# Sliding-window attention and a ReGLU layer: v's second copy by transfers over the sync queue, one more product on GpSimd, and other due times for early work

## The chip, the cores and the metric

The kernel runs on one core of a Trainium2 chip. The metric is the device time of one execution in microseconds (us). Before the change it is 318.4 us, the median of three runs (318.24 to 318.41).

A core has a matrix engine (TensorE, PE in the profile), a vector engine (DVE), an engine for activations (ACT), a general one (GpSimd, POOL in the profile), and a sync engine (SP) that here only issues transfers. Each works through its own queue in order and waits for the others at semaphores. Matrix products land in PSUM, of which there are eight banks of 128 x 512 float32.

## What is computed

Batch 8, 8 heads, 576 positions, head size 64. Every position looks at itself and the 63 before it. The result, 4608 tokens of 512 values, goes through a ReGLU layer of width 1536.

```python
def _attn_ref(q, k, v):
    scores = scale * np.matmul(q, k.transpose(0, 1, 3, 2))
    mask = (rel >= 0) & (rel < 64)
    scores = np.where(mask, scores, -1000000000.0)
    ...
    return np.matmul(attn, v)

def _moe_ref(x, w_gate, w_val, w_out):
    gate = np.maximum(x @ w_gate, 0.0)
    val = x @ w_val
    return gate * val @ w_out
```

## The kernel before

**Tiles.** The 4608 tokens are cut into four narrow tiles of 384 (tiles 0 to 3) and six wide ones of 512 (tiles 4 to 9). For each tile the kernel computes attention, turns it into `xt` (features on partitions), computes the hidden layer into `g_sb`, and multiplies by `wo` into the output, 128 rows at a time.

**The order of the work** is written out by a planner, `Weaver`. It has a clock that is advanced by the estimated time of the matrix products as they are emitted, and a heap of pieces of work with due times: `W.at(t, fn)`. Each `W.advance` emits all that is due. `W.pop` emits the earliest piece before its time, where a product needs its result. So due times set only the order in each engine's queue; on the chip an engine runs an instruction as soon as its queue and its inputs allow. A function that is called from the heap and adds to the clock itself (`scores`, `values` in the heap) leaves no trace in the clock, because `pop` writes back its own sum: the planner's clock falls behind there.

**Attention.** `qk_load` brings q and k of a batch and half of the heads on GpSimd's queue, with a cast to fp16; `qk_trans` transposes them on DVE, 128 x 576 each, four for a batch (names `kT`, `qT`). Each of the four has one staging buffer, so a load waits for the transpose of the batch before. `plan_batch(b, load, trans)` plans both. Narrow tiles have units of 192 positions (`u_st`, `u_exp`, `u_mask`, `u_pv`: scores on TensorE, exp on ACT, mask on DVE, value products on TensorE); `pair` plans the two units of a tile. Wide tiles have quads of four windows (`scores`: scores, exp and mask) and `values` (value products, reciprocal, norm and transpose on DVE, and `x_form`, differences of blocks of `xt`, on GpSimd and DVE). For a wide tile, `values` of the next tile run between the output blocks of this one, and `scores` of the tile after that as well.

**v.** `v16s` holds two batches of v in fp16, in groups of 64 positions, each head with 64 values and two ones (66 in all). A window of 64 queries needs the 128 positions that end with it, so every half of 64 rows is needed at partitions 0 to 63 in one group and at 64 to 127 in another. `v_load` brings each half once (GpSimd's queue, with a cast), and `v_spread` copies it to the other partitions: two copies for each unit of 192 positions, on DVE (units 0 and 3) or GpSimd (all others). `v_ahead` and `loads` plan them.

**Hidden layer, narrow tiles (`hidden`).** Gate and value products into one bank each, ReLU on ACT, multiply on DVE.

**Hidden layer, wide tiles (`fast_hidden`).** Blocks of two by two are multiplied with seven products (P1 to P7) instead of eight, from sums of the weights (`us`, `vs`, made once by `w_form` on GpSimd) and of the inputs (`xc`). Three rounds j of 14 products (seven for the gate, i = 0, and seven for the value, i = 1), 42 steps of four matrix instructions. P1, P6, P7 and P4 add up in one bank A, in this order; after each of the first three `snap` copies the bank to SBUF on ACT (L594), and the next product into A has to wait for this copy. P2, P5 and P3 go to other banks, and `add` sums them to the copies on DVE (L604). P3 waits for the sum with P7. Each finished pair gets a ReLU on ACT (L610) and a multiply on GpSimd (L615). These copies live in six buffers `pr`, each with a gate and a value half, taken in turn: three for a round. The fourth quarter, which is A after P4, goes by `direct`: ReLU on ACT into a buffer `r` (L624), and a multiply on DVE that reads the value half straight from PSUM (L633).

**Output.** `fast_output` multiplies `g_sb` with `wo` for four blocks of 128 rows (12 matrix instructions each, L676), with attention of later tiles between them; ACT copies each block to `o_sb`, and SP writes it out (L683; L699 in narrow tiles). For the first two blocks it reads the half h = 0 of `g_sb`, which has the fourth quarters of each round first.

Of the kernel before, what the change touches and what calls it, by code (L numbers as in the profile page):

```python
# [10 lines left out]
FP32 = mybir.dt.float32  # L11
FP16 = mybir.dt.float16
ACT = mybir.ActivationFunctionType
MUL = mybir.AluOpType.mult
# [33 lines left out]
def kernel(  # L48
# [10 lines left out]
    nc = tc.nc  # L59
# [12 lines left out]
    WT = 512  # L72
    NS = 4
# [12 lines left out]
    f_sb = ctx.enter_context(tc.tile_pool(name="f_sb", bufs=3))  # L86
# [6 lines left out]
    wv = persist.tile([128, NC, DF], FP16)  # L93
    wo = persist.tile([128, NF, DM], FP16)
    HF = NF // 2
# [42 lines left out]
    W = Weaver()  # L138
# [32 lines left out]
    def qk_load(b, name, hh):  # L171

        tile_ = nat[b, name, hh] = a_in.tile([128, S // 32 * D], FP16, name=f"{name}{hh}")
        src = (q if name == "q" else k)[b, G * hh:G * hh + G]
        nc.gpsimd.dma_start(tile_, src.rearrange("h (i j) d -> (h i) (j d)", i=32))
# [14 lines left out]
    def qk_trans(b, name, hh, j0=0, j1=S // 32):  # L190

        src = nat[b, name, hh].bitcast(FP32).rearrange("p (j e) -> p j e", e=32)
        dst = qTs[b % 2][:, hh] if name == "q" else kTs[b % 2][:, hh, 64:64 + S]
        dst = dst.bitcast(FP32).rearrange("p c o -> p (c o)")
        nc.vector.transpose(dst.rearrange("p (i j) -> p j i", i=32)[:, j0:j1], src[:, j0:j1])
# [8 lines left out]
    def v_spread(u, copy=None, h0=0, h1=H):  # L204

        b, uu = divmod(u, UB)
        t = v16s[b % 2]
        copy = copy or nc.vector.tensor_copy
        for g0, g1 in (((0, 3),), ((4, 5),), ((6, 7),))[uu]:
            copy(t[64:128, g0:g1:2, h0:h1, 0:64], t[0:64, g0 + 1:g1 + 1:2, h0:h1, 0:64])  # L210
        for g0, g1 in (((2, 3),), ((4, 5),), ((6, 9),))[uu]:
            copy(t[0:64, g0:g1:2, h0:h1, 0:64], t[64:128, g0 - 1:g1 - 1:2, h0:h1, 0:64])

    def heat(n, to, start=True):

# [57 lines left out]
    def u_st(u, hhs=(0, 1)):  # L273
        d = units.setdefault(u, {})
        if "st" not in d:
            st_tiles(u)
        run_rows([[st_block(d["st"][g][:, U * hh + 64 * w:U * hh + 64 * w + 64], g, hh, UB * u + w, "biased" in d)
                   for hh in hhs for w in range(UB)] for g in range(G)])
        return 0.29 * len(hhs)
# [42 lines left out]
    def u_recip(u, hhs=(0, 1)):  # L322
        d = units[u]
        if "r" not in d:
            d["r"] = a_n.tile([128, 2, SB, 1], FP32, name="r")
        for hh in hhs:
            nc.vector.reciprocal(d["r"][:, hh], pv_of(d, u, hh)[:, :, D:D + 1])
# [36 lines left out]
    free = []  # L364
# [111 lines left out]
    def w_form(wt, n, j):  # L476

        to = us if wt is wg else vs
        c = slice(256 * j, 256 * j + 256)
        f = slice(256 * j + 128 * HF, 256 * j + 128 * HF + 256)  # L480
        a11, a12, a21, a22 = wt[:, 0:2, c], wt[:, 2:4, c], wt[:, 0:2, f], wt[:, 2:4, f]
        x, y, op = ((a21, a22, ADD), (to[:, 0, :, c], a11, SUB), (a11, a21, SUB), (a12, to[:, 1, :, c], SUB))[n]
        nc.gpsimd.tensor_tensor(to[:, n, :, c], x, y, op)

    def plan_batch(b, load, trans):
        for i, (name, hh) in enumerate((n, hh) for n in "kq" for hh in range(2)):
            if load is not None:
                W.at(load, lambda name=name, hh=hh: qk_load(b, name, hh))
            W.at(trans[i], lambda name=name, hh=hh: qk_trans(b, name, hh))

    def plan_exps(T, u, mask=True, gap=0.4, first=0.8):
        for i in range(G):
            W.at(T + first + gap * i, lambda i=i: u_exp(u, i))
            if mask:
                W.at(T + first + 0.45 + gap * i, lambda i=i: u_mask(u, i))
# [54 lines left out]
    def fast_hidden(t):  # L550

        g_sb, done = gs[t] = g_sb_p.tile([128, NF, WT], FP16, name="g_sb"), {}
        xt, xc = xt_tile(t), xcs[t]
        b11, b21, b22 = xt[:, 0:2, 0:HT], xt[:, 2:4, 0:HT], xt[:, 2:4, HT:WT]
        gh = g_sb.rearrange("p f (h n) -> p f h n", h=2)
        pair = lambda ap: ap.rearrange("p (f n) -> p f n", f=2)
        kinds = ((wg, us), (wv, vs))
        at = {}
# [60 lines left out]

        def direct(j, i):  # L620
            if i == 0:
                def relu():
                    at[j, "r"] = f_sb.tile([128, WT], FP32, name="r", bufs=2)
                    nc.scalar.activation(at[j, "r"], at[j, "A", 0], ACT.Relu)  # L624
                    free.append(at[j, "A", 0])
                    at[j, "relu"] = True
                W.at(W.clock, relu)
            else:
                def mult():
                    while (j, "relu") not in at:  # L630
                        W.pop()
                    f = 2 * j + HF
                    nc.vector.tensor_tensor(gh[:, f:f + 2, 0], pair(at[j, "r"]), pair(at[j, "A", 1]), MUL)  # L633
                    free.append(at[j, "A", 1])
                    done[f, 0] = done[f + 1, 0] = True
                W.at(W.clock + 0.2, mult)

        def step(j, name):
            for i in range(2):
# [97 lines left out]
    with tc.manual_schedule():  # L737
        G3, V3, O3 = ([(wt, src, f0, f0 + 4) for f0 in (0, 4, 8)]
                      for wt, src in ((wg, moe_w_gate), (wv, moe_w_val), (wo, moe_w_out)))
        act, dve, pool = nc.scalar.copy, nc.vector.tensor_copy, nc.gpsimd.tensor_copy  # L740
# [81 lines left out]
        def pair(t, TA, TB, P):  # L822
            for u, T in ((2 * t, TA), (2 * t + 1, TB)):
                W.at(T, lambda u=u: u_st(u))
                plan_exps(T, u)
            W.at(P, lambda: u_pv(2 * t) + u_pv(2 * t + 1))
            for n in range(2):
                u = 2 * t + n
                W.at(P + 0.7 + 1.7 * n, lambda u=u: u_recip(u))
                for hh in range(2):  # L830
                    W.at(P + 0.9 + 0.5 * hh + 1.7 * n, lambda u=u, hh=hh: u_norm(u, hh))
                W.at(P + 1.9 + 1.7 * n, lambda u=u: u_turn(u))

        def loads(t, T):
            for u in (2 * t, 2 * t + 1):
                b, uu = divmod(u, UB)
                if uu == 0:
                    plan_batch(b, T - 12.0, (T, T + 1.4, T + 2.8, T + 4.2))
                W.at(T - 6.0, lambda u=u: v_load(u))
                W.at(T + 1.0, lambda u=u: v_spread(u, pool))  # L840

        for u in (4, 5):
            W.at(52.0, lambda u=u: v_spread(u, pool))
        pair(2, 55.5, 58.5, 61.9)
        L_T = 3 * 6.53
        WIDE_T = L_T + 13.1
# [1 line left out]
        def batch_of(t):  # L848
            w0 = q_window(2 * (t - NS), 0)
            b = (w0 + 2 * QW - 1) // NG  # L850
            return b, w0 <= NG * b

        def qk_ahead(t, T, gaps, lead=12.0):
            b, new = batch_of(t)
            if new:
                plan_batch(b, T - lead, [T + x for x in gaps])

        def v_ahead(t, T):
            b, new = batch_of(t)
            us = list(range(UB * b, UB * b + UB)) if new else []  # L860
            if t == NS:
                us.insert(0, UB * b - 1)
            for i, u in enumerate(us):
                W.at(T - 5.0, lambda u=u: v_load(u))
                W.at(T + 6.0 + 2.5 * i, lambda u=u: v_spread(u, pool))

        LAST = NS + NL - 1
        SLOTS = (2.6, 6.53 + 0.8, 6.53 + 2.6, 2 * 6.53 + 0.8)

        def ahead(t):  # L870
            T = W.clock
            if t + 1 < NS:
                pair(t + 1, T + 11.0, T + 14.0, T + 17.5)
            if t == NS - 2:
                qk_ahead(NS, T + 20.5, (0.0, 1.5, 3.0, 4.5))
                v_ahead(NS, T + 27.0)
                for j in range(NF // 4):
                    for n, at in enumerate((0, 1, 3, 2)):
                        W.at(T + 12.0 + 6.4 * j + 1.6 * n, lambda at=at, j=j: w_form(wv, at, j))
            if t == NS - 1:  # L880
                qk_ahead(NS + 1, T + 11.5, (0.0, 1.4, 8.0, 9.4))
                for qd, x in ((0, 6.0), (1, 9.2), (2, 22.6), (3, 25.8)):
                    def st(qd=qd):
                        scores(qd, W.clock, two_banks() + two_banks(), qd == 3)
                    W.at(T + x, st)
                for hh in range(2):
                    def pv(hh=hh):
                        values(NS, hh, W.clock, two_banks() + [one_bank()])
                    W.at(T + 15.7 + 0.1 * hh, pv)
                qk_ahead(NS + 2, T + 27.6, SLOTS, 6.0)  # L890
                v_ahead(NS + 1, T + 27.6)
            if NS <= t:
                if t + 3 <= LAST:
                    qk_ahead(t + 3, T + WIDE_T, SLOTS)
                if t + 2 <= LAST:
                    v_ahead(t + 2, T + WIDE_T)
# [5 lines left out]
        T = 67.0  # L902
# [65 lines left out]
```

## Time and profile before

| view | what it shows |
|---|---|
| runs | 318.4 us median of three (318.24 to 318.41) |
| profiled execution | 318.92 us, span of the instructions 317.2 us, granted clock 0.995 |
| TensorE pauses | 1.1 us in tile 2, 0.2 in tile 3, 1.7 from 123.5 to 158.57 (tile 4) |
| start | TensorE works in 7.97 of the first 15.15 us |
| end | 2.8 us of the last 31.6 without TensorE |

How to read it. All times are us from the start of the span unless ns is said. The profile page has the busy time of the engines, the transfer queues, the chain of work that ended last, and groups of instructions with their idle time before. In a row of a timeline stand start, duration, engine, line, operation, result<-inputs, shape, how many were merged, and in brackets the idle time of the engine before it and what ended it. Matrix instructions are pipelined and their ends are modelled, so four of them show 0.60 us where the next four start 0.437 us later. A row of a table by stage has the stretch, its length, the busy time of each engine with its count of instructions, the granted clock, and the share and rate of the transfer engines.

The chain that ended last gives TensorE 80% of the span, DVE 8%, ACT 4%, transfers and GpSimd 2% each. GpSimd's 44 copies of v take 33.2 us in all; its loads of v 34.7 us of issue.

### The profile page before, as it was taken

What the parts mean: (1) busy time and instruction counts of PE and PEld (TensorE: products, weight loads), DVE (VectorE), ACT (ScalarE), POOL (GpSimd) and SP (SyncE); (2) the same over time, 40 slices, a digit from 0 to 9 for tenths busy, and PEclk for the clock granted to TensorE, in tenths of its full rate; (3) what the DMA queues carried; (4) which work ended last, traced back from release to release, by engine and by line L of the source; (5) the groups of instructions that cost most, each with busy time, mean ns of one, the idle gap of its engine ahead of it and who ended that gap; (6) DMA issues with size and microseconds to landing.
All of it is one profiled execution on the core that took longest, in us unless ns stands there. A gap on an engine that the chain in (4) does not pass through costs nothing.

```text
span 317.2 us, 10104 instructions
## 1 busy us (share of the span) xinstructions
PE 303.1 (96%) x4293; PEld 210.9 (66%) x4293; DVE 237.2 (75%) x433; ACT 181.7 (57%) x364; POOL 212.9 (67%) x236
## 2 busy tenths in 40 slices
PE   4699999999999999999999999999999999999996
PEld 2486958655545555785588648865887588748854
DVE  6936982868895797799969996998588948854840
ACT  3635234532614715983688468755886588618842
POOL 8759759843998609589949983986489416642650
PEclk9989999999999999999999999999999999999999
DMA  7999994946299105910990099002900210020002
GB/s 216 176 196 198 197 147 128 170 111 104 42 139 191 24 15 106 196 12 30 184 148 2 7 211 145 1 2 70 142 0 3 75 61 3 2 102 33 2 33 100
DMA packets 52493, 29.55 MB, mean 93 GB/s; under 512 B 38880, under 2 KB 43872, under 8 KB 52448
## 3 DMA queue, kind: packets, MB, share of 16 engines
q0 software_dynamic: 46688, 18.29, 49.4%
q1 hardware_dynamic: 5616, 10.55, 9.2%
q8 instruction: 33, 0.54, 0.7%
q14 instruction: 12, 0.10, 0.1%
q10 hardware_dynamic: 144, 0.07, 0.1%
HBM read 37.75 MB, written 9.44 MB: 149 GB/s over the span
## 4 chain that ended last, share of the span: by engine, by line
PE 80%; DVE 8%; ACT 4%; DMA 2%; POOL 2%; issue 2%; DVEq 0%; ACTq 0%; POOLq 0%
PE bank L583 27%; PE bank L676 19%; PE bank L541 17%; PE bank L691 10%; DVE pr L604 3%; PE bank L255 3%; PE bank L424 2%; DMA wg<-in_moe_w_gate_dram 2%; DVE p L294 2%; ACT pr L594 2%; ACT pw L391 2%; POOL v L201 1%; DVE g_sb L528 1%; PE bank L721 1%; PE bank L313 1%
## 5 line engine op out<-in xcount | busy, mean ns | idle before, releaser
L615 POOL TENSOR_TENSOR g_sb<-pr 128x512 f16<-128x512 f32 x54 | 68.1, 1277 | 45.0 <-ACT pr L610 42.6
L604 DVE TENSOR_TENSOR pr<-bank,pr 128x512 f32<-128x512 f32 x108 | 68.9, 682 | 24.6 <-PE bank L583 17.2
L594 ACT COPY pr<-bank 128x512 f32<-128x512 f32 x108 | 58.0, 594 | 12.4 <-PE bank L583 8.7
L676 PE MATMUL bank<-wo,g_sb 128*128 128x512 f16 x276 | 62.9, 380 | 0.0
L676 PEld LDWEIGHTS <-g_sb 128*128 128x128 f16 x276 | 25.5, 98 | 28.9
L528 DVE TENSOR_TENSOR g_sb<-pr,bank 128x384 f16<-128x384 f32 x48 | 25.8, 548 | 20.8 <-PE bank L541 19.4
L525 ACT ACTIVATE pr<-bank 128x384 f32<-128x384 f32 x48 | 23.6, 495 | 29.9 <-PE bank L541 20.7
L610 ACT ACTIVATE pr<-pr 128x512 f32<-128x512 f32 x54 | 34.7, 642 | 8.0 <-DVE pr L604 7.8
L541 PE MATMUL bank<-xt,wg 128*128 128x192 f16 (+1 forms) x256 | 36.2, 294 | 1.3 <-DMA wg<-in_moe_w_gate_dram 0.9
L201 POOL DMA_DIRECT2D v<-in_v_dram x41 | 34.7, 872 | 1.8 <-DMA q<-in_q_dram 1.0
L681 ACT COPY o_sb<-bank 128x512 f32<-128x512 f32 x23 | 13.5, 586 | 37.8 <-PE bank L676 35.1
L541 PE MATMUL bank<-xt,wv 128*128 128x192 f16 (+1 forms) x256 | 34.3, 286 | 0.0
L691 PE MATMUL bank<-wo,g_sb 128*128 128x512 f16 x144 | 32.8, 379 | 0.2 <-DVE g_sb L528 0.2
L583 PE MATMUL bank<-xc,vs 128*128 128x256 f16 x216 | 32.4, 272 | 0.4 <-ACT pr L594 0.4
L583 PE MATMUL bank<-xc,us 128*128 128x256 f16 x216 | 32.4, 273 | 0.0
L583 PEld LDWEIGHTS <-vs 128*128 128x128 f16 x288 | 28.1, 98 | 5.7 <-issue 2.5
L583 PEld LDWEIGHTS <-us 128*128 128x128 f16 x288 | 28.1, 98 | 5.1 <-issue 1.6
L541 PEld LDWEIGHTS <-wg 128*128 128x128 f16 x256 | 23.9, 101 | 10.7 <-DMA wg<-in_moe_w_gate_dram 1.4
L396 DVE TENSOR_TENSOR pw<-pw,mask 128x512 f16<-128x512 f16 x48 | 24.2, 533 | 8.7 <-ACT pw L391 8.1
L541 PEld LDWEIGHTS <-wv 128*128 128x128 f16 x256 | 22.9, 98 | 8.1
L391 ACT ACTIVATE pw<-bank 128x512 f16<-128x512 f32 x48 | 26.0, 612 | 1.2 <-PE bank L255 0.8
L461 POOL TENSOR_TENSOR xc<-xt 128x512 f16<-128x512 f16 x12 | 13.9, 1166 | 19.0 <-DVE xt L449 19.0
(78 smaller groups left out, 469.4 us busy)
## 6 DMA issues: line engine op xcount, KB each, us to landing
out_dram<-o_sb SPq DMA_DIRECT2D x35, 256.0 KB, 3.1
k<-in_k_dram POOLq DMA_DIRECT2D x15, 288.0 KB, 5.2
q<-in_q_dram POOLq DMA_DIRECT2D x15, 288.0 KB, 7.7
v<-in_v_dram POOLq DMA_DIRECT2D x31, 128.0 KB, 5.9
wg<-in_moe_w_gate_dram POOLq DMA_DIRECT2D x6, 256.0 KB, 6.8
wv<-in_moe_w_val_dram POOLq DMA_DIRECT2D x6, 256.0 KB, 8.4
wo<-in_moe_w_out_dram POOLq DMA_DIRECT2D x3, 512.0 KB, 11.6
v<-in_v_dram POOLq DMA_DIRECT2D x10, 64.0 KB, 6.1
```

Of the source, the lines that this page charges most:

```text
L201: nc.gpsimd.dma_start(v16s[b % 2][lo:hi, g, :, 0:64], v[b, :, 64 * g - 64 + lo:64 * g - 64 + hi].rearrange("h p d -> p h d"))
L391: nc.scalar.activation(d["p"][g].rearrange("p n c -> p (n c)"), d["st"][g], ACT.Exp, scale=scale)
L396: nc.vector.tensor_tensor(d["p"][g], d["p"][g], mask[:, None, :].to_broadcast([128, 2 * QW, 64]), MUL)
L528: nc.vector.tensor_tensor(g_sb[:, f:f + w, c0:c0 + n], part(r_sb), part(h2), MUL)
L541: nc.tensor.matmul(h[:, b * n:b * n + n], wt[:, c, (f + b) * 128:(f + b) * 128 + 128], xt[:, c, c0:c0 + n], start=(c == 0), stop=(c == NC ...
L583: nc.tensor.matmul(to[:, HT * m:HT * m + HT], w[:, k, 128 * m:128 * m + 128], x[:, k], start=(first and m == 0 and k == 0), stop=(k == 1), ...
L594: nc.scalar.copy(pr[:, i], at[j, "A", i])
L604: nc.vector.tensor_tensor(pr[:, i], to, pr[:, i], ADD)
L610: nc.scalar.activation(pr[:, 0], pr[:, 0], ACT.Relu)
L615: nc.gpsimd.tensor_tensor(gh[:, f:f + 2, h], pair(pr[:, 0]), pair(pr[:, 1]), MUL)
L676: nc.tensor.matmul(op, g_sb[:, f, 128 * sub:128 * sub + 128], wo[:, f], start=(i == 0), stop=(i == NF - 1))
L691: nc.tensor.matmul(op, g_sb[:, f, bass.ds(sub * 128, 128)], wo[:, f], start=(f == 0), stop=(f == NF - 1))
```

## The change

Three things change.

1. `v_spread` without a given copy function issues a transfer on SP's queue instead of a DVE copy; it moves whole rows of 8 x 66 values. Of the calls, those of units 0, 1 and 2 still name an engine; units 3 to 23 go over SP.
2. `direct` takes a pair buffer `pr` for the fourth quarter, ACT copies both halves from PSUM into it (ReLU for the gate, a plain copy for the value), and GpSimd multiplies them. So a round takes four of the six pairs, and bank A is freed by ACT.
3. Due times: the transposes of a narrow batch; `pair` of tile 3, which runs in tile 2 (scores 2.5 us earlier, values 0.2); the loads and copies of v before tile 4; `w_form` of wv; q and k, scores and values in tile 3; and SLOTS, the times of the four transposes in each wide tile.

```diff
     def v_spread(u, copy=None, h0=0, h1=H):
...
-        copy = copy or nc.vector.tensor_copy
+
+        def rows(to, at):
+            if copy:
+                copy(to[:, :, h0:h1, 0:64], at[:, :, h0:h1, 0:64])
+            else:
+                nc.sync.dma_start(to, at)
         for g0, g1 in (((0, 3),), ((4, 5),), ((6, 7),))[uu]:
-            copy(t[64:128, g0:g1:2, h0:h1, 0:64], t[0:64, g0 + 1:g1 + 1:2, h0:h1, 0:64])
+            rows(t[64:128, g0:g1:2], t[0:64, g0 + 1:g1 + 1:2])
         for g0, g1 in (((2, 3),), ((4, 5),), ((6, 9),))[uu]:
-            copy(t[0:64, g0:g1:2, h0:h1, 0:64], t[64:128, g0 - 1:g1 - 1:2, h0:h1, 0:64])
+            rows(t[0:64, g0:g1:2], t[64:128, g0 - 1:g1 - 1:2])
...
         def direct(j, i):
             if i == 0:
-                def relu():
-                    at[j, "r"] = f_sb.tile([128, WT], FP32, name="r", bufs=2)
-                    nc.scalar.activation(at[j, "r"], at[j, "A", 0], ACT.Relu)
-                    free.append(at[j, "A", 0])
-                    at[j, "relu"] = True
-                W.at(W.clock, relu)
-            else:
-                def mult():
-                    while (j, "relu") not in at:
-                        W.pop()
-                    f = 2 * j + HF
-                    nc.vector.tensor_tensor(gh[:, f:f + 2, 0], pair(at[j, "r"]), pair(at[j, "A", 1]), MUL)
-                    free.append(at[j, "A", 1])
-                    done[f, 0] = done[f + 1, 0] = True
-                W.at(W.clock + 0.2, mult)
+                at[j, "r"] = f_sb.tile([128, 2, WT], FP32, name="pr", bufs=6)
+
+            def copy():
+                nc.scalar.activation(at[j, "r"][:, i], at[j, "A", i], ACT.Copy if i else ACT.Relu)
+                free.append(at[j, "A", i])
+                if i == 1:
+                    W.at(W.clock + 0.7, mult)
+
+            def mult():
+                f = 2 * j + HF
+                nc.gpsimd.tensor_tensor(gh[:, f:f + 2, 0], pair(at[j, "r"][:, 0]), pair(at[j, "r"][:, 1]), MUL)
+                done[f, 0] = done[f + 1, 0] = True
+            W.at(W.clock, copy)
...
-                    plan_batch(b, T - 12.0, (T, T + 1.4, T + 2.8, T + 4.2))
+                    plan_batch(b, T - 12.0, (T - 1.5, T, T + 2.4, T + 4.8))
                 W.at(T - 6.0, lambda u=u: v_load(u))
-                W.at(T + 1.0, lambda u=u: v_spread(u, pool))
+                W.at(T + 1.0, lambda u=u: v_spread(u))
 
         for u in (4, 5):
-            W.at(52.0, lambda u=u: v_spread(u, pool))
+            W.at(52.0, lambda u=u: v_spread(u))
...
-                W.at(T + 6.0 + 2.5 * i, lambda u=u: v_spread(u, pool))
+                W.at(T + 6.0 + 2.5 * i, lambda u=u: v_spread(u))
 
         LAST = NS + NL - 1
-        SLOTS = (2.6, 6.53 + 0.8, 6.53 + 2.6, 2 * 6.53 + 0.8)
+        SLOTS = (0.2, 3.4, 7.6, 13.8)
 
         def ahead(t):
             T = W.clock
             if t + 1 < NS:
-                pair(t + 1, T + 11.0, T + 14.0, T + 17.5)
+                pair(t + 1, T + 8.5, T + 11.5, T + 17.3)
             if t == NS - 2:
                 qk_ahead(NS, T + 20.5, (0.0, 1.5, 3.0, 4.5))
-                v_ahead(NS, T + 27.0)
+                v_ahead(NS, T + 20.0)
                 for j in range(NF // 4):
                     for n, at in enumerate((0, 1, 3, 2)):
-                        W.at(T + 12.0 + 6.4 * j + 1.6 * n, lambda at=at, j=j: w_form(wv, at, j))
+                        W.at(T + (1.0, 16.5, 22.9)[j] + 1.6 * n, lambda at=at, j=j: w_form(wv, at, j))
             if t == NS - 1:
-                qk_ahead(NS + 1, T + 11.5, (0.0, 1.4, 8.0, 9.4))
-                for qd, x in ((0, 6.0), (1, 9.2), (2, 22.6), (3, 25.8)):
+                qk_ahead(NS + 1, T + 7.0, (0.0, 3.5, 4.7, 12.0), 6.0)
+                for qd, x in ((0, 3.0), (1, 6.4), (2, 19.0), (3, 22.0)):
                     def st(qd=qd):
                         scores(qd, W.clock, two_banks() + two_banks(), qd == 3)
                     W.at(T + x, st)
                 for hh in range(2):
                     def pv(hh=hh):
                         values(NS, hh, W.clock, two_banks() + [one_bank()])
-                    W.at(T + 15.7 + 0.1 * hh, pv)
+                    W.at(T + 14.2 + 0.1 * hh, pv)
```

## The prediction

> **What bounds the kernel now.** I read the page first, then the trace by stages, then the timeline of each engine in the stages that lost time.
>
> The page's first part gives engine, busy time, share, instructions:
>
> ```profile
> PE 303.1 (96%) x4293; PEld 210.9 (66%) x4293; DVE 237.2 (75%) x433; ACT 181.7 (57%) x364; POOL 212.9 (67%) x236
> ```
>
> TensorE bounds it; only its pauses can be won. Busy time by stage (columns PE, PEld, DVE, ACT, POOL, clock, DMA share, GB/s), for the seven-product stage of tile 5 (first row) and of tile 7 (second):
>
> ```profile
> 158.57:177.90 19.33, 18.82 (x176) 16.23 (x178) 16.19 (x24) 15.84 (x30) 14.51 (x16) 1.00 0.58 63
> 223.85:242.19 18.34, 18.34 (x177) 16.26 (x178) 12.14 (x20) 15.84 (x30) 12.59 (x14) 1.00 0.47 43
> ```
>
> Same matrix work, 18.34 us undisturbed; tile 5 loses 1.0, and so does tile 6 (also 19.33). What differs is DVE: 16.19 against 12.14 us, the four transposes of q and k. TensorE's timeline shows where it pauses:
>
> ```profile
> 122.90 0.60 PE L583 MATMUL bank<-xt,wg 128*128 128x256 f16 x4
> 144.04 0.60 PE L583 MATMUL bank<-xt,us 128*128 128x256 f16 x4 [0.62 <-DVE pr L604]
> 145.17 0.69 PE L424 MATMUL bank<-v,pw 128*32 128x65 f16 x64
> 171.67 0.60 PE L583 MATMUL bank<-xt,vs 128*128 128x256 f16 x4 [0.43 <-DVE pr L604]
> ```
>
> Tile 4's stage runs from 122.90 to 145.17: 22.27, less the 0.62 of one score block inside it, is 21.65; it loses 3.2 us (21.65 - 18.43, the distance of the same two points in tile 7). Half of that falls before 132, while exps and masks of two quads share ACT and DVE with the first products. Tiles 7 to 9 lose nothing. Tile 2 loses 1.1 (pauses of 0.37, 0.22 and 0.53 between 75 and 88), tile 3 0.2. Together 6.5 us are there to be won.
>
> **A. Unit 3's v copies become two transfers.** Removed: DVE's two copies at 43.90 and 44.35 (0.42 + 0.29 us). They lie just before unit 3's value products at 45.10, to which TensorE comes without a pause. SP has nothing ahead of these transfers, so they start when v has landed: its load was issued at 29.78 and took 10.0 us, so 39.8. How long such a transfer takes is not in the trace. The nearest rows are SP's output writes: 256 KB in 2.3 us at 277.76 with idle queues, 7.5 us at 96.52 and 7.7 at 123.76 behind GpSimd's loads. At 39.8 to 46 wo and v are still loading (16 engines over 0.9 busy), so the loaded row is nearer; with 132 and 66 KB instead of 256 I take 6: landing at 45.8 to 46.2, a pause of about 1. The masks ahead matter as well:
>
> ```profile
> 42.98 0.88 DVE L294 TENSOR_TENSOR p<-p,mask 128x384 f16<-128x384 f16 x3
> 80.88 4.38 DVE L294 TENSOR_TENSOR p<-p,mask 128x384 f16<-128x384 f16 x4 [1.05 <-ACT p L289]
> 45.86 0.60 POOL L210 COPY v<-v 64x512 f16<-64x512 f16 x1 [3.47 <-DMA v<-in_v_dram]
> ```
>
> A mask takes 0.3 us beside an idle POOL and 1.1 beside POOL's w_form. Today POOL idles from 42.4 to 45.86 because its copy waits for v; without the copies it goes on with w_form, and three masks at 0.7 (two took 1.42 at 57.30) to 1.1 end at 45.1 to 46.3. The two delays overlap. **A = +1.1**, bounds 0 (the idle row) and +2.8 (7.7 us from 40.2).
>
> Against this the page "DMA: Bandwidth & Descriptors" (Anatomy of one DMA) puts a transfer at about 2.0 us plus bytes over 436 GB/s: as an estimate from it 2.3 us, A nothing. Its fit is for the other issue path and for one transfer alone; the 7.5 and 7.7 us rows show what a full queue adds, and decide here.
>
> **B. All later copies leave POOL.** 40 of its 44 copies go (33.2 us in all, so some 30). POOL is no bound: its products end well before the output needs them in tile 5. The gain is in tile 2. w_form of wv starts there only at 77.7, since POOL stands before q and k loads until the transposes free their tiles, and then collides with the masks (row at 80.88). In the change its first group is due 11 us earlier, transposes 1.5 us earlier, scores 2.5 us earlier, so masks run at about 77 to 82 while POOL issues v loads; masks beside v loads were fast (0.61 for two at 59.11). The 1.1 us of pauses go. **B = -1.1**, bounds 0 and -1.3 (with tile 3's 0.2).
>
> Queues: 21 units' 42 transfers join SP at 0.3 to 0.4 us of issue each. One that waits for v holds the output writes behind it, but in tile 7, say, the last write of the tile before goes out at 224.55, v lands at 229.0 and the next write is at 246.16, so no cost. The value products use them a tile later; that tile is the cover, and without it each would cost what A does.
>
> **C. Tile 4.** The last two score blocks move from 22.6 and 25.8 us after tile 3's start to 19 and 22. Both now run in tile 3's output, where ACT idles (waits of 5.37, 1.96 and 2.77 us between its o_sb copies). Quad 2's exps and masks are then done when tile 4 starts; quad 3's still take the first 2 us. The next transposes' base lies 4.2 us after tile 4's start (27.6 planned against 23.4 by the planner's clock), and the first is due 0.2 behind it instead of 2.6: near 127.3, where k landed at 127.56, so it waits for little. I leave 1.2 us of 3.2. **C = -2.0**, bounds -0.5 (k 1.5 us late, everything on DVE behind it) and -2.8.
>
> **D. DVE in tiles 5 and 6.** Three multiplies of 682 ns leave each tile, and the first transpose falls in the 1.5 us for which DVE waits at the tile's start (158.45 to 159.99). By order of issue, the third then stands before one P1 sum with over half a microsecond of room, so the 0.6 us pause near 171 goes; the fourth still stands before the last P7 sums, so 0.4 near 177 stays. **D = 2 x -0.6 = -1.2**, bounds 0 and -2.0.
>
> **E. ACT's extra copy, all six wide tiles.** Rows by form, with mean ns:
>
> ```profile
> L615 POOL TENSOR_TENSOR g_sb<-pr 128x512 f16<-128x512 f32 x54 | 68.1, 1277 | 45.0 <-ACT pr L610 42.6 <-DVE pr L604 1.3 <-DVE rw L438 0.2
> L594 ACT COPY pr<-bank 128x512 f32<-128x512 f32 x108 | 58.0, 594 | 12.4 <-PE bank L583 8.7 <-POOL g_sb L615 1.2
> L633 DVE TENSOR_TENSOR g_sb<-r,bank 128x512 f16<-128x512 f32 x18 | 12.3, 682 | 4.4 <-ACT r L624 3.4
> ```
>
> 18 products go from DVE (12.3 us) to POOL (18 x 1.277 = 23), with 18 more copies on ACT (18 x 0.594 = 10.7). Per wide tile POOL has 12 products, 14.8 us at the 1.23 apart that back to back pairs show: it fits in 18.34 only without the copies. ACT had 15.84 of 18.34; three more at 0.49 apart make 17.3. In the middle round it is full:
>
> ```profile
> 234.81 0.60 ACT L624 ACTIVATE r<-bank 128x512 f32<-128x512 f32 x1
> 235.30 0.62 ACT L610 ACTIVATE pr<-pr 128x512 f32<-128x512 f32 x1
> 235.82 1.06 ACT L594 COPY pr<-bank 128x512 f32<-128x512 f32 x2
> 237.48 1.07 ACT L594 COPY pr<-bank 128x512 f32<-128x512 f32 x2 [0.60 <-PE bank L583]
> ```
>
> A copy put after the first row moves the third to 236.32, its first half ends at 236.90, and P6, which starts at 236.79 today, waits for it: 0.16 there, 0.2 with its second half. In rounds one and three ACT has room. The pair taken for the direct product must be free too: it is six allocations back, its POOL product ends near 234.75, just before 234.81. The output's use of the third direct product (about 244.6) is over 1 us after POOL's end of it (243.4). **E = 6 x 0.2 = +1.2**, bounds 0 and 6 x 0.6 = +3.6 (a whole copy each, and some 0.1 for the buffer).
>
> The page "SBUF — State Buffer" (Who interferes with whom) says that a DVE instruction with two SBUF inputs and a GpSimd one that reads SBUF shut each other out for a whole instruction. That speaks against the new POOL products beside quad 3's masks in tile 4: one such meeting each would be, as an estimate from it, up to 1.27 us of C. By the row at 80.88 it is 1.1 against 0.3, yet the first product there starts only at 128.97, after those masks are due.
>
> **Sum**, against the profiled execution's 318.92 us (span 317.2 and 1.7 around it): +1.1 - 1.1 - 2.0 - 1.2 + 1.2 = -2.0. The median of the runs is 318.4, 0.5 below that execution; the forecast for it is 318.4 - 2.0 = 316.4, own range 314.9 to 317.7.
>
> **Rivals.**
> - **ACT takes DVE's place (slower).** With a wait s in each wide tile at P6 of the last round, the sum is -3.2 + 6s. It turns slower by 0.2% (0.64 us) from s = 0.64; were a copy late in two rounds plus 0.3 for a pair that POOL holds, s is 0.8: 318.4 - 3.2 + 4.8 = 320.0. For it: ACT at 17.3 of 18.34, six pairs for twelve allocations instead of nine. Against: 0.4 to 0.6 us of idle time in each round today.
> - **The late transfer eats it.** A at +2.8 and C at only -1.7 with D at -0.8: 2.8 - 1.1 - 1.7 - 0.8 + 1.2 = +0.4, so 318.8, or no change if one is milder. For it: wo's load still runs; against: half the bytes of the 7.5 us rows.
> - **Nearly all pauses go.** A = 0, B -1.2, C -2.6, D -1.8, E +0.6: -5.0, 313.4. For it: only tiles 2 to 6 pause. Against: each piece needs its good bound.
> - **Nothing but shifted load:** copies go from an engine that bounded nothing, and the new times change no wait: then only E and A are left, 320.7. The collisions shown above speak against it.
>
> **How the numbers follow.** Chances: forecast 0.47, nearly all pauses gone 0.17, late transfer 0.15, ACT bound 0.16, shifted load 0.05. A change of 0.2% is about what a measurement here can tell. Faster by that: 0.46 + 0.17 = 0.63; within: most of the late transfer, 0.14; slower: 0.23. Range 313.2 to 319.7: outside it are about half of the best case, over half of the ACT case and the shifted load, 2 in 10 together.
>
> **What would show it.** A: TensorE's pause before unit 3's value products near 45 to 46, with the transfers' landing. B: masks of tile 2 at 0.3 us each and no pauses from 75 to 88. C: tile 4's stage near 19.6 us. D: tiles 5 and 6 at 18.9 to 19.0. E: tiles 7 to 9 at 18.5 instead of 18.34, with P6 released by ACT. Wrong if tiles 7 to 9 grow by over 0.6, or if SP's transfers land after their value products.

## The result, and the profile after

The changed kernel takes 316.93 us (median of 20 runs) against 318.43 of the kernel before (20 runs); ratio (of the means) 0.9962, 95% interval 0.9948 to 0.9976. Three of the 20 executions took 319.1 to 319.2 us, the other 17 took 316.6 to 317.4; none of the three was profiled. The profiled execution has a span of 315.0 us against 317.2. This pair differs by 2.2 us, the medians by 1.5: the profiled execution of before is 0.5 above its median, that of the changed kernel 0.2 below.

The first part of the page of the changed kernel (engine, busy time, share, instructions), and from its sixth part the new transfers (count, size of each, median time from issue to landing):

```profile
PE 303.0 (96%) x4293; PEld 211.3 (67%) x4293; DVE 225.4 (72%) x413; ACT 190.0 (60%) x382; POOL 204.6 (65%) x214
```

```profile
v<-v SPq DMA_DIRECT2D x14, 132.0 KB, 3.1
v<-v SPq DMA_DIRECT2D x28, 66.0 KB, 2.6
```

TensorE does the same work, DVE has lost 12 us, ACT gained 8 and POOL lost 8. Busy time by stage of the changed kernel, tile 5's and tile 7's seven-product stages (length, then PE, PEld, DVE, ACT, POOL, clock, DMA share, GB/s):

```profile
155.92:174.91 18.99, 18.87 (x177) 16.24 (x178) 14.91 (x21) 17.26 (x33) 12.46 (x12) 1.00 0.67 87
220.60:239.19 18.59, 18.55 (x177) 16.25 (x178) 10.71 (x17) 16.85 (x33) 12.04 (x12) 1.00 0.59 71
```

Tile 5 has become shorter (19.33 before), tile 7 longer (18.34), with ACT at 17 us in both. To see where the time went I measured the same points of TensorE's timeline in both profiles: the first product of each stage to the first one of the next.

| stretch | before | after | difference | forecast |
|---|---|---|---|---|
| start to unit 3's scores | 40.60 | 40.32 | -0.28 | 0 |
| unit 3: scores to the output after its values | 4.99 | 6.09 | +1.10 | A +1.1 |
| from there to tile 2 | 22.48 | 22.51 | 0 | 0 |
| tile 2 | 27.59 | 25.62 | -1.97 | B -1.1 |
| tile 3 and tile 4's products | 49.51 | 47.97 | -1.54 | C -2.0, E +0.2 |
| tiles 5 and 6, products | 38.85 | 38.17 | -0.68 | D -1.2, E +0.4 |
| tiles 7 to 9, products | 55.20 | 55.97 | +0.77 | E +0.6 |
| outputs between, and the end | 77.98 | 78.38 | +0.40 | 0 |

Together -2.2 us, the difference of the spans. The first and the last row hold chance: over the fourteen profiles of this document the stretch up to unit 3's scores ranges from 39.48 to 41.19 us, and what comes behind tile 9's products, where 0.34 of the last row's 0.40 lies, from 13.40 to 14.21.

Unit 3, TensorE's timeline, then DVE's, and last DVE's rows of the eight masks of tile 2, all of the changed kernel (in brackets the pause and what ended it):

```profile
45.25 0.21 PE L318 MATMUL bank<-v,p 128*32 128x65 f16 x3 [0.35 <-DMA v<-v]
45.86 0.62 PE L318 MATMUL bank<-v,p 128*32 128x65 f16 x45 [0.40 <-DVE p L299]
```

```profile
42.50 3.30 DVE L299 TENSOR_TENSOR p<-p,mask 128x384 f16<-128x384 f16 x3
79.24 0.74 DVE L299 TENSOR_TENSOR p<-p,mask 128x384 f16<-128x384 f16 x2 [0.40 <-ACT p L294]
80.36 0.62 DVE L299 TENSOR_TENSOR p<-p,mask 128x384 f16<-128x384 f16 x2
81.83 1.89 DVE L299 TENSOR_TENSOR p<-p,mask 128x384 f16<-128x384 f16 x4 [0.39 <-ACT p L294]
```

The first pause is the transfer, the second the last mask: both late, one behind the other. Before, the same three masks took 0.88. In tile 2 it is the other way round: the first unit's four masks took 4.38 before, beside GpSimd's sums of weights, and now 0.74 and 0.62, beside its loads. TensorE has no marked pause there.

The middle of tile 7, ACT's timeline and TensorE's:

```profile
231.62 1.08 ACT L630 ACTIVATE pr<-bank 128x512 f32<-128x512 f32 x2
232.59 0.63 ACT L615 ACTIVATE pr<-pr 128x512 f32<-128x512 f32 x1
233.10 1.08 ACT L599 COPY pr<-bank 128x512 f32<-128x512 f32 x2
```

```profile
233.10 0.60 PE L588 MATMUL bank<-xt,vs 128*128 128x256 f16 x4
233.74 0.60 PE L588 MATMUL bank<-xc,us 128*128 128x256 f16 x4
```

Steps of TensorE start 0.437 apart; these two are 0.64 apart. The second is P6 of the last round, and the first copy of P1 (233.10, 0.59 long) has ended at 233.69.

Tile 3's last score block in the changed kernel, TensorE:

```profile
120.95 0.40 PE L260 MATMUL bank<-qT,kT 32*128 32x64 f16 x29 [0.27 <-ACT pw L396]
121.54 0.42 PE L260 MATMUL bank<-qT,kT 32*128 32x64 f16 x32 [0.19 <-DVE qT L195]
```

It has to wait for the exps of the block before and for q's second transpose. Tile 4's products take 19.30 instead of 21.65 (22.27 less the score block inside them), but this block now stands in tile 3, which gives 0.8 of it back.

### The profile page after: what moved, and what is told of

It is laid out like the page before. It is cut to its first block, busy times and chain, and to the rows that moved or that the text cites. A ratio compares the mean times of both kernels' runs of the same rounds, so it can differ in the third digit from the quotient of the medians.

```text
span 315.0 us, 10191 instructions
## 1 busy us (share of the span) xinstructions
PE 303.0 (96%) x4293; PEld 211.3 (67%) x4293; DVE 225.4 (72%) x413; ACT 190.0 (60%) x382; POOL 204.6 (65%) x214
## 4 chain that ended last, share of the span: by engine, by line
PE 83%; DVE 6%; ACT 4%; POOL 2%; DMA 2%; issue 1%; DVEq 0%; ACTq 0%; POOLq 0%
PE bank L588 29%; PE bank L546 20%; PE bank L679 20%; PE bank L694 7%; PE bank L260 3%; PE bank L429 2%; DMA wg<-in_moe_w_gate_dram 2%; DVE pr L609 2%; DVE p L299 1%; ACT pr L599 1%; DVE qT L195 1%; POOL v L201 1%; ACT pr L615 1%; PE bank L318 1%; PE bank L724 1%
## 5 line engine op out<-in xcount | busy, mean ns | idle before, releaser
L609 DVE TENSOR_TENSOR pr<-bank,pr 128x512 f32<-128x512 f32 x108 | 69.6, 684 | 37.7 <-PE bank L588 31.4
L401 DVE TENSOR_TENSOR pw<-pw,mask 128x512 f16<-128x512 f16 x48 | 22.6, 501 | 5.5 <-ACT pw L396 4.7
```

Source lines behind the costliest of these rows:

```text
L609: nc.vector.tensor_tensor(pr[:, i], to, pr[:, i], ADD)
```

## The experiments

All times are medians; the kernel before ran beside each set: 318.29 in the first, 318.45 in the second, 318.24 in the third.

### The parts taken singly

**Due times alone.** v's copies and the multiply as before; the due times stay changed.

```diff
-                W.at(T + 1.0, lambda u=u: v_spread(u))
+                W.at(T + 1.0, lambda u=u: v_spread(u, pool))
...
-        W.at(43.0, lambda: v_spread(3))
+        W.at(43.0, lambda: v_spread(3, dve))
```

(and the same at the other calls; `direct` as in the kernel before)

> Due times of the changed kernel; v's copies on GpSimd (unit 3 on DVE) and the fourth quarter's multiply on DVE as before. Theory (the due times carry the gain; transfers and the product on GpSimd cost time at unit 3 and at P6): 315.9 us, unit 3's pause gone, tiles 7 to 9 back at 18.34 to 18.43, tile 2 near 25.8. Rival (the parts need each other: GpSimd's copies push the moved work late again): 317.5 or more, tile 2 near 27 and tile 4 above 20.5.

Measured: 316.34 us, ratio 0.9941 (0.9919 to 0.9963), runs from 315.4 to 317.9. The profiled execution is the longest of the ten, 317.91. In it tiles 2 to 9 are as good as the theory says or better (tile 2 25.62, tile 4's products 19.04, tiles 5 and 6 18.83, 7 to 9 18.34 to 18.43), and unit 3 is back at 4.99. But 4.5 us are lost where neither theory looked: from unit 3 to tile 2, 27.04 instead of 22.5; the other executions, which were up to 2.5 us shorter, probably lost less. In kind it is what the rival said, GpSimd's copies push other work late. From the chain that ended last (start, us, what), and GpSimd's timeline there:

```profile
60.53 4.87 DVE p L299 x4
```

```profile
60.42 1.20 POOL L488 TENSOR_TENSOR us<-wg 128x512 f16<-128x512 f16 x1
61.53 1.31 POOL L488 TENSOR_TENSOR vs<-wv 128x512 f16<-128x512 f16 x1
62.92 1.15 POOL L488 TENSOR_TENSOR vs<-vs,wv 128x512 f16<-128x512 f16 x1
```

Unit 5's four masks take 1.2 us each, because GpSimd, held up by its copies, gets to the sums of wv just then. In the changed kernel these sums are over at 60.2. So the due times carry the gain of tiles 2 to 6, but the sums' earlier time needs GpSimd free of the copies.

**The multiply back on DVE**, transfers and due times as changed (`direct` as in the kernel before).

> The changed kernel with the fourth quarter's multiply back on DVE, read from PSUM, all else as changed. Theory (ACT's extra copy costs 0.25 us in each of six tiles, DVE's relief gives some 0.3 in tiles 5 and 6 and little in tile 4): 316.0 us, P6 without its wait, tiles 7 to 9 at 18.4, tiles 5 and 6 near 19.1. Rival (DVE's relief is what gives tiles 4 to 6 their gain): 317.5 or more, tiles 5 and 6 back at 19.4 and tile 4 above 20.5.

Measured: 315.56 us, 0.9919 (0.9902 to 0.9935): faster than the whole change. Tile 4's products 19.04, tiles 5 and 6 18.83, tiles 7 to 9 18.34 to 18.43: each 0.25 less than in the changed kernel, and nothing is lost on DVE. The third part is a loss in every wide tile. Its unit 3 stretch is 7.16 us, by the transfer (TensorE):

```profile
45.68 0.31 PE L318 MATMUL bank<-v,p 128*32 128x65 f16 x16 [1.55 <-DMA v<-v]
46.35 0.43 PE L318 MATMUL bank<-v,p 128*32 128x65 f16 x32 [0.37 <-DMA v<-v]
```

**The copies back on GpSimd**, the multiply on GpSimd and due times as changed (the calls as in the first experiment).

> The changed kernel with v's copies back on GpSimd (unit 3 on DVE), products of the fourth quarter on GpSimd. Theory (GpSimd then has 14.8 us of products and 4.5 of copies in an 18.4 us stage, and a product that ends late holds a pair that ACT waits for): unit 3's 1.1 us come back as a gain, tiles 4 to 7 lose 0.5 or more each, 317.0 to 318.0 us. Rival (GpSimd is off the path either way): 315.9 us, tiles 4 to 7 as in the changed kernel.

Measured: 331.17 us, 1.0421 (1.0374 to 1.0467): the theory's sign, at more than ten times the size. The products' stages are untouched (19.08 in tiles 5 and 6). The outputs behind tiles 4 to 7 take 17.64, 15.48, 17.09 and 15.80 instead of 13.16 to 13.26, 13.1 us in all in the profiled execution (333.47 us, the longest of four), and the stretch before tile 2 is 26.74 as in the first experiment. TensorE and GpSimd behind tile 5:

```profile
187.84 1.04 PE L679 MATMUL bank<-wo,g_sb 128*128 128x512 f16 x4 [2.10 <-POOL g_sb L637]
```

```profile
182.32 1.68 POOL L211 COPY v<-v 64x512 f16<-64x512 f16 x2
184.08 2.49 POOL L620 TENSOR_TENSOR g_sb<-pr 128x512 f16<-128x512 f32 x2
186.52 1.26 POOL L637 TENSOR_TENSOR g_sb<-pr 128x512 f16<-128x512 f32 x1
```

The output needs the fourth quarter of the last round, and this product is the last but two of GpSimd's queue, behind the copies. What waits is the output, not, as I expected, ACT for a pair.

**The due times of before**, with transfers and the multiply on GpSimd.

```diff
-        SLOTS = (0.2, 3.4, 7.6, 13.8)
+        SLOTS = (2.6, 6.53 + 0.8, 6.53 + 2.6, 2 * 6.53 + 0.8)
```

(and all the other due times)

> Transfers over SP and the product on GpSimd as changed, all due times as before. Theory (due times carry the gain): 319.5 to 320.3 us, above the kernel before: unit 3 pauses for 0.7 to 1.1 us, tile 2 keeps 27 us or more, tiles 7 to 9 lose 0.25 each. Rival (the relief of DVE and GpSimd carries it): 317.0 us.

Measured: 320.59 us, 1.0074 (1.0057 to 1.0090). Unit 3 takes 6.69, tile 2 27.55, tiles 5 and 6 19.42 as before the change, tiles 7 to 9 18.6 to 18.69. Parts one and two alone cost 2.3 us. They do give something back in tile 4, 21.50 instead of 22.27, and in tiles 5 and 6 too, if P6 waits there as in tiles 7 to 9: they stay as they were.

### The costs by themselves

**One ACT copy moved.** The changed kernel, with the value half's copy of the middle round behind P1's copies.

```diff
-            W.at(W.clock, copy)
+            W.at(W.clock + 0.9 * (j == 1 and i == 1), copy)
```

> The changed kernel with one ACT instruction moved: the value half's copy of the fourth quarter in the middle round is due 0.9 us later, behind both copies of P1. Theory (P6 of the last round waits because this copy stands before P1's): tiles 7 to 9 go from 18.69 to 18.4 us, all six tiles gain 0.25, 315.5 us. Rival (ACT is simply full, or a pair buffer is held): the wait moves to another product and the time stays at 316.9.

Measured: 315.33 us, 0.9904 (0.9887 to 0.9921). Tiles 4 to 9: 19.04, 18.83, 18.83, 18.43, 18.43, 18.34: all six lose their 0.25. ACT in tile 7:

```profile
232.02 0.62 ACT L615 ACTIVATE pr<-pr 128x512 f32<-128x512 f32 x1
232.54 1.06 ACT L599 COPY pr<-bank 128x512 f32<-128x512 f32 x2
233.48 0.62 ACT L630 ACTIVATE pr<-bank 128x512 f32<-128x512 f32 x1
```

The same work in another order: ACT isn't full, and no pair is held. Moving this copy is as good for these stages as putting the multiply back.

**GpSimd's sums away from unit 3's masks.** Loads of q, k and v for tile 3's batch ahead of the second group of weight sums.

```diff
-                    plan_batch(b, T - 12.0, (T - 1.5, T, T + 2.4, T + 4.8))
-                W.at(T - 6.0, lambda u=u: v_load(u))
+                    plan_batch(b, T - 27.5, (T - 1.5, T, T + 2.4, T + 4.8))
+                W.at(T - 27.0, lambda u=u: v_load(u))
```

> The changed kernel with the loads of q, k and v for tile 3 put before the second group of weight sums on GpSimd, so that GpSimd issues loads while DVE masks unit 3. Theory (mask and GpSimd sum shut each other out): the three masks take 0.9 us instead of 3.3, and unit 3's value products wait for the transfers alone, landing 5.8 us after issue: 0.3 to 0.5 us less, 316.5 us. Rival (the transfers end last in any case, and more loads make them later): masks fast, time 316.9 or more.

Measured: 321.58 us, 1.0099 (1.0083 to 1.0114). DVE's row of the three masks, GpSimd's next load, and the chain at the transfer:

```profile
41.51 0.89 DVE L299 TENSOR_TENSOR p<-p,mask 128x384 f16<-128x384 f16 x3
43.11 0.53 POOL L175 DMA_DIRECT2D q<-in_q_dram  x1 [2.24 <-DMA wo<-in_moe_w_out_dram]
```

```profile
40.65 7.36 DMA v<-v
```

The masks are fast, as the theory says. They run beside no sum, and beside no issuing either: from 40.87 to 43.11 GpSimd waits for a transfer of wo. But the transfer among more loads takes 7.4 us instead of 5.9, the stretch is 8.89, and the sums, now later, meet the masks of units 4 and 5: 25.17 to tile 2, 2.7 more. Mechanism shown, remedy bad.

**Unit 3's copies on DVE again.**

```diff
-        W.at(43.0, lambda: v_spread(3))
+        W.at(43.0, lambda: v_spread(3, dve))
```

> The changed kernel with unit 3's two copies of v on DVE again, behind its masks. Theory (the masks beside GpSimd's sums are late as well): masks end at 45.8 and 0.7 us of copies follow, the pause before unit 3's values stays at 1.4 to 1.8 us, 317.2 us. Rival (the late transfer alone makes the pause): the pause goes, 315.9 us.

Measured: 319.39 us (317.65 to 320.82), 1.0026 (1.0006 to 1.0045), slower than either theory. From the chain, and GpSimd's timeline behind its sums:

```profile
42.26 3.30 DVE p L299 x3
45.58 0.52 DVE v L211
46.13 1.13 DVE v L211
```

```profile
45.29 1.14 POOL L175 DMA_DIRECT2D k<-in_k_dram  x2
46.41 1.08 POOL L175 DMA_DIRECT2D q<-in_q_dram  x2
```

The masks run beside GpSimd's sums, the last of which ends at 45.34. The copies take 1.65 us instead of 0.71, and beside them GpSimd runs no sum, it issues the loads of k and q; that this holds the copies up is likely, but not shown. The stretch is 8.17, against 6.09 to 7.27 in the profiles with the transfers and the same sums. So the transfers don't make unit 3's pause alone: with GpSimd busy, DVE copies are worse than transfers. The profiled run is the fastest of its twelve; what makes the others longer was not looked into.

**The sums of wv at their old due times.**

```diff
-                        W.at(T + (1.0, 16.5, 22.9)[j] + 1.6 * n, lambda at=at, j=j: w_form(wv, at, j))
+                        W.at(T + 12.0 + 6.4 * j + 1.6 * n, lambda at=at, j=j: w_form(wv, at, j))
```

> The changed kernel with the sums of wv at their due times of before (12.0, 18.4 and 24.8 us after tile 2's start instead of 1.0, 16.5 and 22.9). Theory (the gain of 2.0 us in tile 2 is the masks getting out of the way of GpSimd's sums): tile 2 goes from 25.6 to 27 us or more, masks there take 0.6 to 1.1 us, 318.0 us or more. Rival (the earlier scores and transposes alone make the gain): tile 2 stays below 26, 316.9 us.

Measured: 317.35 us, 0.9981 (0.9959 to 1.0003); tile 2 takes 25.75 us, as the rival has it. But this run doesn't put the masks back beside the sums. DVE and GpSimd in tile 2:

```profile
83.33 2.33 DVE L299 TENSOR_TENSOR p<-p,mask 128x384 f16<-128x384 f16 x2 [0.27 <-ACT p L294]
```

```profile
80.52 5.82 POOL L201 DMA_DIRECT2D v<-in_v_dram  x7
```

After two sums GpSimd issues the loads of v, whose earlier due time was kept, up to 86.3. Only the masks at 79.58 (1.47 us for two) meet a sum. The two slow masks shown run beside the loads, and TensorE doesn't wait for them: the scores come 2.5 us earlier, so there is room before the values. Whether sums beside these masks would still cost time in tile 2 stays open.

### Mends put together

**First try.** The multiply on DVE, unit 3 on DVE, the early loads, and SLOTS with 17.0 in place of 13.8.

```diff
-        SLOTS = (0.2, 3.4, 7.6, 13.8)
+        SLOTS = (0.2, 3.4, 7.6, 17.0)
```

> The changed kernel with the fourth quarter's multiply on DVE, unit 3's copies on DVE, the early loads of tile 3, and the last of the four transposes of a wide tile due 3.2 us later, behind the sums that P3 of the last round waits for. Theory: unit 3's pause goes (1.1 to 2.2 us against the kernel with the multiply on DVE, 315.56), tiles 5 and 6 lose their 0.4 us: 313.2 us, tiles 5 and 6 at 18.5. Rival (one pause takes the place of another): 315 us or more.

Measured: 318.77 us (316.01 to 319.93), 1.0010 (0.9990 to 1.0030). Unit 3 is at 4.99 and tiles 5 and 6 at 18.43, so the pause before P3 of the last round is gone. More than that is lost from unit 3 to tile 2, 28.00 us instead of 22.51; from the chain there:

```profile
62.44 4.45 DVE p L299 x4
```

The sums again, on unit 5's masks.

**Units 3 to 5 as before, and the sums of wv in GpSimd's waiting time** between the loads of k and q.

```diff
-                W.at(load, lambda name=name, hh=hh: qk_load(b, name, hh))
+                W.at(load + 0.01 * i, lambda name=name, hh=hh: qk_load(b, name, hh))
...
-                        W.at(T + (1.0, 16.5, 22.9)[j] + 1.6 * n, lambda at=at, j=j: w_form(wv, at, j))
+                        W.at(T + (8.515, 16.5, 22.9)[j] + (1.6 * n if j else 0.001 * n), lambda at=at, j=j: w_form(wv, at, j))
```

(`v_spread(3, dve)`, and `pool` for units 4 and 5)

> The changed kernel with unit 3's copies on DVE and units 4 and 5's on GpSimd as before, so that GpSimd stands before v's load while unit 3 is masked; the first four sums of wv then go between k's and q's loads of tile 3's batch, where GpSimd waits. Theory (unit 3 costs 1.1 to 2.2 us, by masks and transfer together, and the sums have a free place after unit 5's masks): stretch of unit 3 back at 5.0 us, stretch to tile 2 at 22.5, tile 2 at 25.6, 315.3 us. Rival (the sums meet masks elsewhere): 316.9 us or more, one of these stretches longer by a microsecond or more.

Measured: 315.08 us, 0.9907 (0.9893 to 0.9920). Unit 3 at 4.99, to tile 2 23.21, tile 2 25.62. The theory holds but for 0.7 us to tile 2.

**All mends**: the same, with the late copy and SLOTS ending in 17.0.

> As the run with unit 3 as before, with the value half's copy of the middle round behind P1's copies, and the last of the four transposes of a wide tile 3.2 us later. Theory (the three are separate: 1.6 us at unit 3, 6 x 0.25 at P6, 2 x 0.4 at P3): 313.0 us, tiles 5 to 8 at 18.4. Rival (they share waits): 314.5 us or more.

Measured: 313.05 us, 0.9835 (0.9821 to 0.9848): faster than both kernels, and at the sum of the three. Tiles 5 to 9 take 18.34 to 18.43, the undisturbed length.

**q's second transpose earlier in tile 3.**

```diff
-                qk_ahead(NS + 1, T + 7.0, (0.0, 3.5, 4.7, 12.0), 6.0)
+                qk_ahead(NS + 1, T + 7.0, (0.0, 3.5, 4.7, 6.2), 6.0)
```

> As the run with all mends, with q's second transpose for tile 5 due 5.8 us earlier in tile 3. Theory (tile 3's last score block waits for this transpose, behind the turns of the values, and DVE has room before them): tile 3 goes from 28.7 to 28.3 us, 312.6 us. Rival (it then delays the gates or the values): 313.0 us or more.

Measured: 313.13 us, 0.9842 (0.9825 to 0.9858). Tile 3 goes from 28.67 to 28.32 in the profiles, as expected; the wait for the transpose is gone and the one for the exps stays:

```profile
120.08 0.66 PE L260 MATMUL bank<-qT,kT 32*128 32x64 f16 x61 [0.27 <-ACT pw L396]
```

The medians don't show it; 0.35 us is too little for four runs, and in the two profiles the start alone differs by 0.8.

## Why the prediction was right, step by step

The forecast of 316.4 us lies 0.5 below the measured 316.93, and the likeliest case is the one that came. The sum of -2.0 stands against -2.2 in the profiled pair and -1.5 in the medians. That it comes so near is in part luck: in the profiled pair tile 2 won 0.9 us more than forecast and the start 0.3 that nobody forecast, and the other rows of the table came out 0.95 us worse together.

- **A, unit 3: right, and it varies.** +1.10 in the profiled execution, both causes as described; the landing was 5.8 and 5.9 us after issue, where I took 6. In the other profiled executions with these transfers and sums the stretch was 6.69 to 7.27, so A is +1.1 to +2.3 (lower bound 0, upper +2.8). Of the two rules, the row of output writes told what loads under way do. The formula of the Trainium skill, "DMA: Bandwidth & Descriptors", Anatomy of one DMA, from which 2.3 us is an estimate, is given for transfers that GpSimd issues; it fits the transfers here that run with few loads beside them (landing after 1.9 to 3.2 us in tiles 4 to 7) and is off by 2.5 times at unit 3.
- **B, tile 2: sign right, size wrong, the reason not fully shown.** -1.97 instead of -1.1, because I summed the pauses that the timeline marks and not the distance of equal points; modelled ends and short waits within merged rows hide the rest. The masks left the sums as forecast (the first unit's four took 4.38 us, now 0.74 and 0.62) and the pauses went. But the run with the sums at their old times doesn't bring the collision back, since the earlier loads of v lie between, and its tile 2 takes 25.75. Which of the earlier scores, transposes, sums and loads of v does the most was not separated. The collision does cost time elsewhere: from unit 3 to tile 2, 4.5 us in the profile of the due times alone and 5.5 in that of the first try.
- **C, tiles 3 and 4: right in kind.** Tile 4 won 2.35, with its score block counted out. The step that failed is that the score block which moves into tile 3's output was put at no cost there: it waits for exps and for q, 0.8 us.
- **D, tiles 5 and 6: right size, wrong author.** Products went from 19.42 to 19.08, with E's 0.25 in it, so D is -0.6 for each tile. But the multiply back on DVE leaves -0.6 in place (18.83): with the transposes' new times DVE's relief adds nothing. The pause of 0.4 before P3 of the last round stayed, as forecast, and went when its transpose was moved.
- **E, ACT: right to 0.05 us.** 0.25 in each of six tiles where I had 0.2, at the forecast product, for the forecast reason; one moved copy takes it back.

The rivals: "ACT takes DVE's place" is the mechanism of E, at 0.25 and far from the 0.64 at which it would decide. "Shifted load" is what parts one and two would be without the new times, 320.59 against my 320.7. That the products would fit on GpSimd only without the copies was told, but not what it is worth: 331 us without the transfers. So part two needs part one and is a loss, which a 0.9 us later copy undoes; the gain is that of the due times. The parts don't simply add up: the due times alone won 2.0 us, parts one and two alone lost 2.3, and all together won 1.5. The transfers keep GpSimd free for the sums' new time; the due times with the transfers take 315.56 us, without them 316.34, and the intervals of the two overlap. Part one by itself was not run.

## What to carry to other kernels

- When work moves to an engine that has room on average, look for the one queue place where its order matters: a copy of 0.59 us put ahead of the one that TensorE waits for cost 0.25 us in every tile, and behind it nothing.
- Taking away a wait on a helper engine lets it run ahead into someone else's time. GpSimd's wait for v protected the masks of unit 3; each remedy that moved its sums moved the collision to other masks, until they were put where GpSimd has to wait anyway.
- Measure a stage between two equal points, not by the pauses that a timeline marks.

## What the runs showed of the hardware

- **Masks on DVE are held by GpSimd's sums.** A mask (fp16, both inputs in SBUF) takes 0.3 us alone and 1.1 to 1.2 beside GpSimd's sums, about one mask for each sum (3.30 for three, 4.87 for four); the sums lose little, 1.15 us alone and 1.31 at most in the rows above. The Trainium skill, "SBUF — State Buffer", Who interferes with whom, says of DVE instructions with two SBUF inputs that they contend with GpSimd instructions that read SBUF, and of copies that they can contend under further conditions. The masks agree.
- **Beside GpSimd's issuing of loads most masks were fast, but not all.** In tile 2 of the changed kernel two masks took 0.62 us (at 80.36) and the next four 1.89; with wv's sums at their old times two took 2.33. What makes the difference is open. Two copies of v on DVE took 1.65 us instead of 0.71 while GpSimd issued loads of k and q.
- **Transfers within SBUF** landed after 1.9 to 3.2 us where few loads run, and after 5.3 to 7.8 beside GpSimd's loads (changed kernel; up to 9.2 with the multiply back on DVE). With few loads 132 KB take some 0.4 us longer than 66 KB (2.4 against 1.9 at 137); beside loads the queue counts, and no difference by size shows.
- **A load on GpSimd's queue can wait until an older one of another tensor has landed:** with the early loads, q's waited 2.24 us for wo's, while the transfer engines were full.
